# Windowed attention and a gated MLP on one core: the start-up rebuilt around keys that lie four rows to a partition

## The chip, the cores and the metric

The kernel runs on one core of a Trainium2 chip. A core has a matrix engine (TensorE, "PE" in the profile; its weight loads are shown apart as "PEld"), a vector engine (DVE), a scalar engine (ACT), GpSimd (POOL) and a queue engine (SP). [...] The metric is device time in microseconds. Three runs of the kernel before gave 316.60, 316.82 and 317.05 us; the median is 316.82 us.

## The reference

Two stages. The first is attention with 8 batches and 8 heads of 64: per head 512 local rows and 32 global rows. Global queries see all 544 keys; a local query sees the 32 global keys and the local keys at most 32 rows away.

```python
s_g = scale * np.matmul(q_g, k_all.transpose(0, 1, 3, 2))
out_g = np.matmul(sm(s_g), v_all)
s_ll = scale * np.matmul(q_l, k_l.transpose(0, 1, 3, 2))
mask = np.abs(pos[:, None] - pos[None, :]) <= 32
s_ll = np.where(mask, s_ll, -1e9)
s_lg = scale * np.matmul(q_l, k_g.transpose(0, 1, 3, 2))
out_l = np.matmul(sm(np.concatenate([s_lg, s_ll], axis=-1)), np.concatenate([v_g, v_l], axis=2))
```

The second takes the 8 x 544 = 4352 rows of 512 values through `h = x @ w_in` (512 to 2048), `g = h * sigmoid(1.702 h)` and `g @ w_out` (2048 to 512).

## The kernel before, in words

**Tiling.** Four heads of one batch form a quad (`class Quad`, L231), one head on each group of 32 partitions; there are 16 quads, two to a batch (called `a` and `c` in the code). A quad's steps are: `Tk` and `Tq` (L249, L256) transpose keys and queries on DVE in 32x32 blocks; `ext` (L264) puts the 32 global queries beside the local ones; `S(rnd)` (L281) makes the scores of key chunks 0, 1 (round 0) or 2, 3 (round 1), each chunk being 128 keys against the window of queries that can see them; `X(rnd)` (L318) is the exponential on ACT; `M(rnd)` (L329) multiplies with a 0/1 mask on DVE; `K` and `XK` (L334, L358) do the same for the global keys; `ekU(unit)` and `U(unit)` (L362, L385) sum, over keys, the row sums (unit 0) and the two halves of the values (units 1, 2); `R` (L416) turns the row sums into reciprocals on DVE; `XL(h)` (L426) scales; `Gm` and `G` (L400, L429) make the global rows' output.

**MLP.** `h_step(i, fc)` (L474) is four 512-column matmuls of batch i into PSUM, a tanh on ACT and one DVE pass into `gT`; `o_mm` (L481) multiplies with `w_out`. After the start-up PE alternates between `h_step`s of one batch and `phase_o`, which mixes that batch's `o_mm`s with the attention of the next.

**Order.** The order of the work is written out by hand (`manual_schedule`): every engine runs its instructions in the order of the code and waits on semaphores that the framework sets from the data. One further limit: a POOL DMA waits for the eighth one before it to have landed. PSUM has one set of four score banks (`psS`, one buffer) and four single banks (`psP`), so a second `S` in the score banks waits for the `X` of the first.

**Start-up, L119 to L602.** Quad 0's keys and queries come in f32 as four 256 KB loads on the ACT and SP queues (L125 to L127) and are converted on ACT (L520) and DVE (L531); quad 1's come through POOL (L149). Keys lie 16 rows to a partition, and `Tk` writes them with a stride so that the transposed keys are in natural order. PE starts with 40 filler matmuls (L163). The window is not applied by `M` here but by `B` (L272): 32 matmuls of an identity with a table of 0 and -262144 put the bias into the banks before `S` adds the scores. The 0/1 mask for later quads is made on ACT between `h_step`s (L599). Values of the global keys (`g32v`) are loaded on SP only after a DVE memset (`hold`, L109) that stands behind the transposes. `load_rest` (L203) issues the rest from POOL: values of batch 0, `w_in` in six pieces (the first 512 columns first), two of the four pieces of `w_out`, then queries, keys and global rows of quad 2, the other `w_out` pieces, and so on.

**Lines the change touches:** `kf`, `vf` (L65, L66), `load` (L73), `load_g32` (L107), the constants (L131 to L149), `make_mask` (L188), `load_rest`, `Tk`, `B`, `S`, `X`, `M`, and the start-up order from L519 to L616.

Of the kernel before, what the change touches and what calls it, by code (L numbers as in the profile page):

```python
# [12 lines left out]
F32 = mybir.dt.float32  # L13
BF16 = mybir.dt.bfloat16
# [6 lines left out]
def kernel(  # L21
# [43 lines left out]
    kf = k_l.rearrange("b (u j) (r t) d -> b (j r) u (t d)", j=4, t=16)  # L65
    vf = v_l.rearrange("b h (c g r) d -> b g r h c d", c=4, g=4)  # L66
# [6 lines left out]
    def load(b, us=(0, 1), kq=True):  # L73
        if b not in loaded:
            loaded[b] = (ld.tile([128, 2, 16 * D], BF16, name="rk"),
                         ld.tile([128, 2, 16 * D], BF16, name="rq"))
        if kq:
            s = slice(us[0], us[-1] + 1)
            nc.gpsimd.dma_start(out=loaded[b][0][:, s], in_=kf[b][:, s])
            nc.gpsimd.dma_start(out=loaded[b][1][:, s], in_=qf[b][:, s])  # L80
# [3 lines left out]
    def load_v(b, us=(0, 1)):  # L84
        s = slice(us[0], us[-1] + 1)
        hs = slice(4 * us[0], 4 * us[-1] + 4)
        for g in range(4):
            p = slice(32 * g, 32 * g + 32)
            nc.gpsimd.dma_start(out=vtiles[b % 2][p, s, :, :, :D], in_=vf[b, g][:, hs])  # L89
# [17 lines left out]
    def load_g32(name, src, hold=False):  # L107
        t = g32[name] = consts.tile([128, 2, D], F32, name="g32%s" % name)
        if hold:  # L109
            nc.vector.memset(t[:, :, 0:1], 0.0)  # L110
        if name == "v":
            load_turned(nc.sync, t, src[:, 0:2, :])
        else:
            nc.sync.dma_start(out=t, in_=src[:, 0:2, :])

    def cast_g32(name, t):
        nc.vector.tensor_copy(t[:, 0:2, :D], g32[name])  # L117

    load(0, kq=False)  # L119
    rk, rq = loaded[0]  # L120
    k32 = ld.tile([128, 16 * D], F32, name="k32", bufs=1)
    q32 = ld.tile([128, 16 * D], F32, name="q32", bufs=1)
    halves = (slice(0, 8 * D), slice(8 * D, 16 * D))
    load_g32("q", qgf)
    for eng, f in ((nc.scalar, halves[0]), (nc.sync, halves[1])):  # L125
        eng.dma_start(out=k32[:, f], in_=kf[0][:, 0, f])
        eng.dma_start(out=q32[:, f], in_=qf[0][:, 0, f])  # L127
    load_g32("k", kgf)


    step = consts.tile([128, 257], BF16)  # L131
    nc.vector.memset(step, 1.0)
    ones32 = consts.tile([128, 32], BF16)
    nc.gpsimd.memset(ones32, 1.0)
    nc.gpsimd.memset(rvg[:, :, D:], 1.0)
    bd = consts.tile([128, 4, 32], BF16)
    nc.gpsimd.memset(bd, 0.0)
    for j in range(4):
        r = (j + 1) % 4
        nc.gpsimd.memset(bd[32 * r : 32 * r + 32, j, :], 1.0)  # L140
    for i in range(2):
        v = consts.tile([128, 2, 4, 4, D + 2], BF16, name="v%d" % i)
        nc.gpsimd.memset(v[:, :, :, :, D:], 1.0)
        vtiles.append(v)
    nc.gpsimd.affine_select(
        out=step, in_=step, pattern=[[1, 257]], compare_op=ALU.is_ge,
        fill=0.0, base=-65, channel_multiplier=-1,
    )
# [14 lines left out]
    keep(40, psP.tile([128, 512], F32, name="w", tag="p"), 128)  # L163
# [8 lines left out]
    WIN = ((0, 10), (6, 12), (14, 12), (22, 10))  # L172
    mask = consts.tile([128, 2, LW], BF16)


    ident = consts.tile([128, 128], BF16)
    band = consts.tile([128, 192], BF16)
    bias = consts.tile([128, 16, 12], BF16)
    bandt = band.rearrange("p (r t) -> p t r", t=16)
    nc.vector.tensor_sub(ident, step[:, 65:193], step[:, 64:192])  # L180
    nc.vector.tensor_sub(band, step[:, 65:257], step[:, 0:192])
    nc.vector.tensor_scalar(bias, bandt, -1.0, 262144.0, op0=ALU.add, op1=ALU.mult)

    def near(t, c):
        lo = 0 if c else 2
        return t[:, :, lo : lo + WIN[c][1]]

    def make_mask(c):  # L188
        nr = WIN[c][1]
        at = (0, 160, 0, 192)[c]  # L190
        nc.scalar.activation(mask[:, c // 2, at : at + 16 * nr].rearrange("p (t r) -> p t r", t=16),
                             near(bandt, c), AF.Copy)
# [10 lines left out]
    def load_rest():  # L203
        vp = v_l[0].rearrange("(u h) (c p) d -> u p h c d", u=2, p=128)
        for u in range(2):
            for p in (slice(0, 64), slice(64, 128)):
                nc.gpsimd.dma_start(out=vtiles[0][p, u, :, :, :D], in_=vp[u, p])
        half = d_ff // 2
        for part, lo, hi in ((0, 0, 512), (0, 512, half), (1, 0, half)):
            for u in range(2):  # L210
                nc.gpsimd.dma_start(out=w_in_sb[:, part, 2 * u : 2 * u + 2, lo:hi],
                                    in_=w_in_r[u][:, :, part * half + lo : part * half + hi])
        for g4 in (1, 0, 2, 3):
            nc.gpsimd.dma_start(
                out=w_out_sb[:, 4 * g4 : 4 * g4 + 4, :].rearrange("p (g e) m -> p g (e m)", e=2),
                in_=w_out_r[:, 2 * g4 : 2 * g4 + 2, :])
            if g4 == 0:
                load(1, (0,))
                load_g(2, 4)
# [11 lines left out]
    class Quad:  # L231
        def __init__(self, Q):
# [11 lines left out]
            self.bk = {}  # L244
# [4 lines left out]
        def Tk(self, lo=0, hi=16):  # L249
            if lo == 0:  # L250
                self.kT = att.tile([128, Sl], F32, name="kT", bufs=3)
                self.k = self.kT.bitcast(BF16).rearrange("p (m e) -> p m e", e=2)
            nc.vector.transpose(self.kT.rearrange("p (r t) -> p t r", t=16)[:, lo:hi],  # L253
                                loaded[self.b][0][:, self.u].bitcast(F32)[:, 32 * lo : 32 * hi])
# [16 lines left out]

        def B(self, rnd, split=False):  # L272
            self.bk[rnd] = [pbank("s") for _ in range(4)] if split else self.spt(rnd)
            ps = self.bk[rnd] if split else [self.bk[rnd][:, j, :] for j in range(4)]
            for c in (2 * rnd, 2 * rnd + 1):
                w = (40, 200, 36, 228)[c]
                for j in range(4):
                    nc.tensor.matmul(ps[j][:, w : w + 16 * WIN[c][1]], lhsT=ident, rhs=near(bias, c),
                                     start=(c == 2 * rnd), stop=False, skip_group_check=True)

        def S(self, rnd, split=False, added=False, part=None):  # L281
            if not added:
                self.bk[rnd] = self.spt(rnd)
            ps = self.bk[rnd] if split else [self.bk[rnd][:, j, :] for j in range(4)]
            for c in (2 * rnd, 2 * rnd + 1):
                off = (0, 200, 0, 228)[c]
                r0, nr = WIN[c]
                t0, t1 = ((0, 20), (4, 23), (1, 20), (4, 24))[c]
                lo, hi = ((t0, t1) if part is None else (12, t1) if part else (t0, 12))
                off += (lo - t0) * nr  # L290
                n = (hi - lo) * nr
                for e in range(2):
                    for j in range(4):
                        p = slice(32 * j, 32 * j + 32)
                        nc.tensor.matmul(  # L295
                            ps[j][:, off : off + n],
                            lhsT=self.k[p, 128 * c : 128 * c + 128, e],
                            rhs=self.q[p, lo:hi, r0 : r0 + nr, e],
# [484 lines left out]
```

## Time and profile before

| what | value |
|---|---|
| median of three runs | 316.82 us |
| profiled execution, its own time | 316.6 us |
| span of its instructions | 314.9 us |
| PE busy | 302.8 us, 96% |
| DVE busy / ACT busy / POOL busy | 210.5 / 167.5 / 55.9 us |
| PE idle in one piece, 13.19 to 16.33 us | 3.14 us |
| first `h_step` matmul of the dense part (fc = 4) | 26.68 us |
| DMA bytes, mean rate | 27.60 MB, 88 GB/s |
| software queue | 45760 packets, 47.7% of 16 engines' span |

The profile is of one execution; its own time is its span plus 1.7 us around it. "PE busy" is the time in which a matmul is in the array. The chain of waits is followed back from the last instruction: each piece is what released the next one. In it PE has 88% of the span, in two lines above all: L488 (`w_out`, 37%) and L463 (`w_in`, 34%). The "timeline" gives instructions in order of time, and in brackets how long the engine was idle before and who ended that. A table "by stretches" gives the busy time of each engine between two times, the TensorE clock that was granted (1.00 is full) and the DMA rate.

### The profile page before, as it was taken

To read this page: it belongs to the slowest core of one execution; us is meant where nothing else is said; L and a number is where in the kernel's file an instruction comes from. 1 tells how busy PE (TensorE), PEld (TensorE's weight loads), DVE (VectorE), ACT (ScalarE), POOL (GpSimd) and SP (SyncE) were. 2 spreads that over 40 slices of the span, in tenths; PEclk is the share of its full clock that TensorE was granted. 3 is DMA by queue.
4 is the path that set the end of the run, shared out by engine and by line. 5 is a ranking of instruction groups with operands and counts; after the bars stand their busy time and mean duration, and the time that the engine had idled before them with its cause. 6 is when DMAs were issued, how large, how long until landed. Compare 5 with 4: busy or idle time off the path is not lost.

```text
span 314.9 us, 7824 instructions
## 1 busy us (share of the span) xinstructions
PE 302.8 (96%) x3272; PEld 149.9 (48%) x3272; DVE 210.5 (67%) x447; ACT 167.5 (53%) x251; POOL 55.9 (18%) x90
## 2 busy tenths in 40 slices
PE   8599999899999999999999999999999999999994
PEld 7354444444454454544554454444454454446553
DVE  6367865696867767678767876776857865573320
ACT  3725746267355655566546744665456642563421
POOL 8533575630004000500032000300000000000000
PEclk9979999999999999999999999999999999999999
DMA  7999999999139511990159312900211012200222
GB/s 194 176 209 206 202 116 189 213 197 94 33 70 120 115 34 37 104 164 3 44 79 158 60 34 60 111 0 18 53 38 32 2 35 52 51 0 18 51 67 68
DMA packets 53923, 27.60 MB, mean 88 GB/s; under 512 B 42496, under 2 KB 43776, under 8 KB 53888
## 3 DMA queue, kind: packets, MB, share of 16 engines
q0 software_dynamic: 45760, 16.95, 47.7%
q1 hardware_dynamic: 7648, 9.51, 12.2%
q10 hardware_dynamic: 480, 0.66, 0.7%
q8 instruction: 25, 0.41, 0.6%
q14 instruction: 10, 0.08, 0.1%
HBM read 35.13 MB, written 8.91 MB: 140 GB/s over the span
## 4 chain that ended last, share of the span: by engine, by line
PE 88%; DVE 4%; DMA 4%; ACT 2%; issue 0%; ACTq 0%; SPq 0%; DVEq 0%
PE op L488 37%; PE hp L463 34%; PE s L295 6%; PE ov L394 5%; PE ov L372 3%; DMA g32v<-in_v_g_dram 2%; DMA k<-in_k_l_dram 1%; DVE gT L471 1%; PE s L463 1%; PE kb L314 1%; PE op L500 1%; PE s L314 1%; ACT th L470 1%; PE s L412 1%; ACT e L325 1%; DVE kT L253 0%
## 5 line engine op out<-in xcount | busy, mean ns | idle before, releaser
L488 PE MATMUL op<-w_out_sb,gT 128*128 128x512 bf16 x528 | 122.0, 380 | 0.1
L471 DVE SCALAR_TENSOR_TENSOR gT<-th,hp 128x512 bf16<-128x512 f32 (+1 forms) x140 | 91.2, 656 | 43.5 <-ACT th L470 42.6
L463 PE MATMUL hp<-xL,w_in_sb 128*128 128x512 bf16 x496 | 109.0, 379 | 1.0 <-DVE xL L427 1.0
L470 ACT ACTIVATE th<-hp 128x512 f32<-128x512 f32 (+1 forms) x140 | 79.9, 573 | 43.6 <-PE hp L463 39.6
L463 PEld LDWEIGHTS <-w_in_sb 128*128 128x128 bf16 x576 | 56.0, 98 | 66.0 <-issue 2.2
L488 PEld LDWEIGHTS <-gT 128*128 128x128 bf16 x528 | 49.2, 98 | 56.4 <-issue 3.5
L325 ACT ACTIVATE e<-s 128x1712 bf16<-128x1712 f32 x31 | 49.5, 1597 | 19.3 <-PE s L412 8.9
L502 ACT ACTIVATE ob<-op 128x512 f32<-128x512 f32 (+2 forms) x35 | 20.5, 585 | 63.1 <-PE op L488 60.6
L89 POOL DMA_DIRECT2D v<-in_v_l_dram x32 | 23.8, 753 | 124.1 <-PE s L412 114.4
L332 DVE TENSOR_TENSOR e<-e,mask 128x1408 bf16<-128x1408 bf16 x28 | 24.4, 871 | 6.7 <-ACT e L325 6.7
L418 DVE STREAM_TRANSPOSE sT<-ov 128x512 f32<-128x512 f32 x15 | 10.7, 716 | 27.1 <-PE ov L394 27.1
L295 PE MATMUL s<-q,kT 32*128 32x228 bf16 (+5 forms) x528 | 21.3, 283 | 0.8 <-DVE q L267 0.8
L427 DVE TENSOR_TENSOR xL<-ov,rs 128x512 bf16<-128x512 f32 x30 | 19.4, 687 | 2.7 <-PE ov L394 1.4
L295 PEld LDWEIGHTS <-kT 32*128 32x128 bf16 x528 | 11.0, 96 | 14.3 <-issue 10.3
L253 DVE STREAM_TRANSPOSE kT<-rk 128x512 f32<-128x512 f32 (+1 forms) x17 | 16.8, 990 | 1.2 <-ACT rk L521 1.2
L360 ACT ACTIVATE ek<-kb 128x512 bf16<-128x512 f32 x16 | 9.6, 602 | 8.0 <-PE kb L314 8.0
L372 PE MATMUL ov<-ek,rvg 32*32 32x512 bf16 x120 | 9.8, 384 | 3.1 <-DVE rvg L117 3.1
L394 PE MATMUL ov<-e,v 128*32 128x160 bf16 (+1 forms) x480 | 12.6, 243 | 0.0
L422 DVE STREAM_TRANSPOSE rs<-rT 128x512 f32<-128x512 f32 x16 | 11.4, 711 | 0.6
L394 PEld LDWEIGHTS <-v 128*32 128x32 bf16 x512 | 10.1, 98 | 1.6 <-issue 1.6
L257 DVE STREAM_TRANSPOSE q<-rq 128x512 f32<-128x512 f32 (+1 forms) x17 | 10.8, 641 | 0.0
L314 PE MATMUL kb<-q,kgT 32*32 32x512 bf16 x128 | 10.0, 385 | 0.0
(77 smaller groups left out, 163.3 us busy)
## 6 DMA issues: line engine op xcount, KB each, us to landing
out_dram<-ob SPq DMA_DIRECT2D x132, 64.0 KB, 1.7
v<-in_v_l_dram POOLq DMA_DIRECT2D x28, 128.0 KB, 4.8
rk<-in_k_l_dram POOLq DMA_DIRECT2D x6, 512.0 KB, 8.5
rq<-in_q_l_dram POOLq DMA_DIRECT2D x6, 512.0 KB, 10.5
w_out_sb<-in_moe_w_out_dram POOLq DMA_DIRECT2D x4, 512.0 KB, 11.5
w_in_sb<-in_moe_w_in_dram POOLq DMA_DIRECT2D x4, 256.0 KB, 9.7
w_in_sb<-in_moe_w_in_dram POOLq DMA_DIRECT2D x2, 512.0 KB, 12.8
rk<-in_k_l_dram POOLq DMA_DIRECT2D x3, 256.0 KB, 7.9
```

The lines of the kernel that those rows point to most:

```text
L89: nc.gpsimd.dma_start(out=vtiles[b % 2][p, s, :, :, :D], in_=vf[b, g][:, hs])
L295: nc.tensor.matmul(ps[j][:, off : off + n], lhsT=self.k[p, 128 * c : 128 * c + 128, e], rhs=self.q[p, lo:hi, r0 : r0 + nr, e], start=(e == ...
L325: nc.scalar.activation(e[:, :, :RW], self.ps[:, :, :RW], AF.Exp, scale=scale)
L332: nc.vector.tensor_mul(e, e, mask[:, rnd : rnd + 1, :].to_broadcast([128, 4, LW]))
L372: nc.tensor.matmul(ov[32 * j : 32 * j + 32, :], lhsT=lv, rhs=self.ek[p], start=True, stop=False, skip_group_check=True)
L394: nc.tensor.matmul(ov[32 * j : 32 * j + 32, :].rearrange("p (t r) -> p t r", t=16)[:, :, r0 : r0 + nr], lhsT=lv, rhs=self.E[c // 2][:, j, ...
L427: nc.vector.tensor_mul(self.x[:, 2 * self.u + h, :], self.st[1 + h], self.st["rs"])
L463: nc.tensor.matmul(hp[:, : width(i)], lhsT=w_in_c[:, fc // 8, kc, fc % 8 // 2, :, fc % 2], rhs=(xL[i] if i < B else xG)[:, kc, :], start=( ...
L470: nc.scalar.activation(th[:, :n], hp[:, :n], AF.Tanh, scale=0.851)
L471: nc.vector.scalar_tensor_tensor(gTs[i][:, fc, :n], in0=th[:, :n], scalar=1.0, in1=hp[:, :n], op0=ALU.add, op1=ALU.mult)
L488: nc.tensor.matmul(op, lhsT=gTs[i][:, fc, tci * 128 : tci * 128 + 128], rhs=w_out_sb[:, fc, :], start=(first and fc == 4 * f4), stop=(fc = ...
L502: nc.scalar.activation(ob[:, lo:hi], op[:, lo:hi], AF.Copy, scale=0.5)
```

## The change

The keys are laid out four rows to a partition in each chunk of 128 (`kf`), so that `Tk` writes without a stride and the transposed keys are in the order (chunk, row mod 4, row div 4). The values take the same order (`vf`), and the mask is built for it. Every key load becomes four DMAs of 32 partitions from POOL instead of one of 128.

In the start-up, `B` with its 32 matmuls goes, and with it the identity and the bias table. Quads 0 and 1 are masked by `M` on DVE, as all later quads were before; quad 1's round 1 has its `X` in two pieces and its `M` in two. The mask is now made ahead of the first `X`: two selects on POOL, four copies on DVE (`make_mb`), four ACT instructions (`make_mask`). Quad 0's keys come through POOL as the first four DMAs, in bf16; its queries as one 512 KB load on ACT's queue, followed there by `g32v`, now without a hold. Several memsets go from POOL to DVE. PE has 62 filler matmuls at the start and 4, 3 and 4 wider ones before `S(1)`, `ekU(1)` and `ekU(2)`. `S` is no longer cut in two for quad 0. Global rows of quads 2 and 3 come in f32 on SP and are converted on ACT in the middle of the first `h_step`s, instead of four DMAs from POOL; their transposes move there as well. `w_in` comes in four pieces instead of six, and `w_out` in natural order.

```diff
-    kf = k_l.rearrange("b (u j) (r t) d -> b (j r) u (t d)", j=4, t=16)
-    vf = v_l.rearrange("b h (c g r) d -> b g r h c d", c=4, g=4)
+    kf = k_l.rearrange("b (u j) (c r t) d -> b j r u c (t d)", j=4, c=4, t=4)
+    vf = v_l.rearrange("b h (c r t) d -> b t r h c d", c=4, t=4)
...
         if kq:
-            s = slice(us[0], us[-1] + 1)
-            nc.gpsimd.dma_start(out=loaded[b][0][:, s], in_=kf[b][:, s])
-            nc.gpsimd.dma_start(out=loaded[b][1][:, s], in_=qf[b][:, s])
+            for j in (0, 2, 1, 3):
+                for u in us:
+                    load_k(b, u, j)
+            load_q(b, us)
+
+    def load_k(b, u, j):
+        nc.gpsimd.dma_start(out=loaded[b][0][32 * j : 32 * j + 32, u], in_=kf[b, j][:, u])
...
-    load_g32("q", qgf)
-    for eng, f in ((nc.scalar, halves[0]), (nc.sync, halves[1])):
-        eng.dma_start(out=k32[:, f], in_=kf[0][:, 0, f])
-        eng.dma_start(out=q32[:, f], in_=qf[0][:, 0, f])
-    load_g32("k", kgf)
+    nc.scalar.dma_start(out=q32, in_=qf[0][:, 0])
+    load_g32(0, "qk")
+    load_g32(0, "v", eng=nc.scalar)
+    for j in range(4):
+        load_k(0, 0, j)
+
+    mk = consts.tile([32, 208], BF16)
+    nc.vector.memset(mk, 1.0)
+    for sg, base in ((1, 2 * W + 3), (-1, -3)):
+        nc.gpsimd.affine_select(
+            out=mk, in_=mk, pattern=[[-sg, 208]], compare_op=ALU.is_ge,
+            fill=0.0, base=base, channel_multiplier=4 * sg,
+        )
     load(0, (1,))
...
-    keep(40, psP.tile([128, 512], F32, name="w", tag="p"), 128)
+    keep(62, psP.tile([128, 512], F32, name="w", tag="p"), 128)
...
+    def make_mb():
+        for k in range(4):
+            nc.vector.tensor_copy(mb[32 * k : 32 * k + 32],
+                                  mk[:, 3 - k : 195 - k].rearrange("p (r t) -> p t r", t=16))
...
     def load_rest():
...
-        for part, lo, hi in ((0, 0, 512), (0, 512, half), (1, 0, half)):
+        load_v(0)
+        for part in range(2):
+            cs = slice(part * (d_ff // 2), (part + 1) * (d_ff // 2))
             for u in range(2):
...
-        for g4 in (1, 0, 2, 3):
+        for g4 in range(4):
...
-            if g4 == 0:
+            if g4 == 1:
                 load(1, (0,))
-                load_g(2, 4)
...
-            nc.vector.transpose(self.kT.rearrange("p (r t) -> p t r", t=16)[:, lo:hi],
-                                loaded[self.b][0][:, self.u].bitcast(F32)[:, 32 * lo : 32 * hi])
+            rk = loaded[self.b][0][:, self.u].bitcast(F32).rearrange("p c w -> p (c w)")
+            cs = slice(128 * cs[0], 128 * cs[-1] + 128)
+            nc.vector.transpose(self.kT[:, cs], rk[:, cs])
...
+    make_mb()
+    cast_q(0)
+    cast_q(1)
+    make_mask()
+    cast_g32(0, "q")
     transpose_g(0, 2, "q")
     a.ext((0, 1))
-    a.Tk(0, 8)
-    a.Tk(8, 16)
-    nc.vector.tensor_copy(rq[:, 0, halves[1]], q32[:, halves[1]])
     a.Tq(0, 8)
     a.Tq(8, 16)
+    a.Tk((0, 1))
     a.ext((2, 3))
-    load_g32("v", vgf, hold=True)
-    cast_g32("k", rkg)
+    a.Tk((2, 3))
+    cast_g32(0, "k")
     transpose_g(0, 2, "k")
     load_rest()
-    a.B(0)
-    a.B(1, split=True)
-    a.S(0, added=True, part=0)
-    a.S(0, added=True, part=1)
+    a.S(0)
     a.X(0)
-    a.S(1, split=True, added=True)
+    a.S(1, split=True, warm=4)
     a.X(1)
+    c.ext()
+    cast_g32(0, "v")
     c.Tk()
-    c.ext()
-    c.Tq()
-    cast_g32("v", rvg)
-    c.B(0)
     a.K()
     a.XK()
-    c.S(0, added=True)
+    a.M(0)
+    c.Tq()
     c.gg()
+    c.S(0)
     c.X(0)
+    a.M(1)
+    load_g32(1, "qkv", hold=True)
     a.eg()
-    c.K()
+    c.K(0)
+    a.ekU(0)
+    c.K(1)
     c.XK()
-    a.ekU(0)
     a.U(0)
     a.R()
-    a.ekU(1)
+    a.ekU(1, 3)
+    c.S(1)
+    c.X(1, halves=True)
+    a.ekU(2, 4)
     a.U(1)
+    a.U(2)
+    a.Gm()
+    c.M(0)
     a.XL(0)
-    c.B(1)
-    c.S(1, added=True)
-    c.X(1)
-    a.ekU(2)
-    a.U(2)
+    c.M(1, 0, 192)
+    c.M(1, 192)
     a.XL(1)
-    a.Gm()
...
-        if fc in (5, 6, 8, 9):
-            make_mask((5, 6, 8, 9).index(fc))
+        if fc == 7:
+            cast_g32(1, "qkv")
+        if fc == 10:
+            transpose_g(2, 4)
...
     a.T()
-    transpose_g(2, 4)
     a.ext()
```

## The prediction

> **What bounds the kernel now.** The page first: is one engine full, and where is it not?
>
> ```profile
> PE 302.8 (96%) x3272; PEld 149.9 (48%) x3272; DVE 210.5 (67%) x447; ACT 167.5 (53%) x251; POOL 55.9 (18%) x90
> ...
> PE   8599999899999999999999999999999999999994
> ```
>
> PE is full but for the first two slices of 7.9 us and the last. Then the table by stretches:
>
> ```profile
> core 0: us, PE busy (x) PEld busy (x) DVE busy (x) ACT busy (x) POOL busy (x), PEclk, DMA share, GB/s
> 8.00:16.00 8.00, 4.12 (x124) 2.36 (x112) 2.37 (x10) 5.95 (x9) 4.41 (x7) 1.00 1.90 176
> 16.00:23.00 7.00, 6.67 (x145) 3.75 (x146) 4.79 (x10) 1.60 (x1) 2.51 (x4) 0.76 1.16 208
> 27.00:37.00 10.00, 10.00 (x48) 4.51 (x47) 8.52 (x13) 8.84 (x17) 5.54 (x9) 1.00 1.20 206
> 131.00:165.00 34.00, 34.00 (x384) 16.12 (x383) 25.13 (x51) 19.70 (x28) 4.12 (x7) 1.00 0.55 78
> ```
>
> From 27 us PE has no gap to speak of, and the change leaves its work there alone: the time is the moment at which the dense part starts, plus a constant. From 8 to 16 us half of PE's time is idle, and after it the granted clock is 0.76: the idle stretch was paid twice. The chain says what set the start, with its beginnings and lengths in us:
>
> ```profile
> 8.62 7.33 DMA g32v<-in_v_g_dram
> 16.05 0.24 DVE rvg L117
> 16.33 0.40 PE ov L372 x4
> ...
> 17.14 0.95 PE s L278 x8
> 18.10 0.83 PE s L295 x13
> ...
> 22.91 3.56 PE s L463 x16
> ...
> 26.75 10.47 PE hp L463 x48
> ```
>
> A 64 KB load of the global values, issued at 8.62 because of its hold, lands at 15.95 behind the bulk loads; all of DVE's queue (`R` of quad 0 too) and PE's `ekU(1)` stand behind it. The timeline gives two more anchors: when quad 1's row sums start, and the one later stall that belongs to key transposes.
>
> ```profile
> 20.93 0.49 PE L394 MATMUL ov<-e,ones 128*32 128x160 bf16 x16
> ...
> 70.61 0.67 PE L295 MATMUL s<-q,kT 32*128 32x200 bf16 x16 [0.76 <-DVE q L267]
> ```
>
> From 20.93 (`c.U(0)`) to the dense part at 26.68 lie 5.75 us of the same instructions in both kernels. So the question is when `c.U(0)` can start: it needs quad 1's second mask product.
>
> **The first scores.** *Queries.* Four 256 KB loads landed at 3.54, 5.11, 5.54 and 6.76; with the two 64 KB ones 1.13 MB were in at 6.97. The changed kernel has 0.70 MB on these queues (512 KB, three times 64), so by proportion from 1.3 us they are in at 4.8, `g32v` with them. Two conversions at 0.63 (L521): 6.1. Four mask instructions at 0.49 to 0.55: 8.1, free while ACT has no scores to read; without that cover they cost up to their 2.1 us. They leave the `h_step`s, where ACT has 8.84 of 10 us and PE no gap: nothing gained there; the three conversions put in their place (about 0.3 each) are less than what left.
> *POOL.* Four key pieces from 0.80 at 0.55 to 0.69 each (L79), then two selects at no more than 0.40 (L145): mask base at 3.8 to 4.4. The memsets taken from POOL (1.1 us) are about as long on DVE, which was waiting anyway. Four copies at about 0.25 (row L181), conversion, transpose and two `ext` (0.23, 0.24, 0.28): 6.2 at the latest. `Tq` in halves at 0.42: 6.5.
> *Keys.* The last piece is issued at 2.45. How long until it lands is the one unknown that matters. Lower bound 3.5 us (a 128 KB value piece on a quiet queue, issued 93.75), upper bound 8.7 (the value piece issued at 5.99, queued behind others); the first software load here took 5.9 beside 1.13 MB of other loads. I take 4.7, midway between 3.5 and 5.9 since less runs beside it: 7.2. First half of `Tk` without stride, as `Tq` 0.42: scores could start at 7.7. The 62 fillers from 1.53 at 111 ns (40 took 4.45) end at 8.4, or at 7.8 if the clock rises at 7.2 as it seems to do here. I take 8.2.
>
> [...]
>
> **From the first scores to `c.U(0)`.** `S(0)` 0.66 (row at full clock): first `X` at 8.9, where before it was 8.53. Then ACT is the bound, in order: 1.60, quad 0's split `X` 1.81, `XK` 0.65, quad 1's `X` 1.60 with 0.19, its `XK` 0.60, a wait of 0.15 as `c.S(1)` (0.66) needs the score banks, and two half `X` together 1.70: 17.3 us. On DVE the added `M`s cost 0.89 each: quad 0's (12.4 to 13.3) stands ahead of `U(0)` and `R` (1.7), all while ACT is busy; quad 1's first at 15.6; `c.Tq`, moved behind a mask product, ends near 12.3, ahead of `c.X(0)`'s turn at 13.05. What is late next: `XL(0)` must have `U(1)`, which stands behind the four fillers (0.86) after `c.S(1)`: done 17.3, so `XL(0)` to 18.0 (0.69), then the two last pieces of `M` (0.49 and 0.41): 18.95. `c.U(0)` at 19.0, 1.9 us sooner than 20.93. No gap of PE on the way is longer than about 1 us, so I count no half clock. `c.R` now starts behind `XL(1)` at 19.6 and ends the second `XL` at 22.8; the matmuls that need it come at 23.5.
>
> The 32 bias matmuls that go (2.09 for 16, 0.77 and 1.02) count nothing beyond this: the first 24 stood under waits, the last 8 under the path just replaced. The 11 wide fillers stand where PE waits for ACT.
>
> **The loads behind.** POOL has 13 DMAs ahead of `w_in` instead of six, so the last value piece is issued near 9.4 (5.99 before) and the second `w_in` piece near 10.5. But these landings were paced by the transfers, not by the issue: `w_in`'s first half was whole at 20.64; its first piece is now wanted at 20.8, its second at 22.7. The keys move as 512-byte packets instead of 2 KB; bytes are equal. Bound below: no wait; above: lags as long as the longest here, 8.7 for values (18.1 against a use at 16.9) and 13.5 for `w_in` (24.0 against 22.7), at most 1.3 us. I take 0, as the transfers are the same but for order. `w_out`, quads 2 and 3 were 2 to 9 us early, and the four POOL DMAs of global rows are gone there (each waited 0.7 to 1.8 us for its turn). Their f32 loads on SP come at about 14, are wanted after 27, and land 7.3 us later as `g32v` did.
>
> **Later.** Key transposes fall from 1.04 to 0.67 (rows kT and q of 128x512). PE waits for DVE only in places; the 0.76 at 70.61 has one such transpose in DVE's backlog before it: 0.37 less, bounds 0 and 0.37, I take 0.35. Seven more POOL DMAs per batch, at 0.55, find POOL 18% busy.
>
> **Sum.** 316.6 (the profiled run) - 1.9 - 0.35 = 314.35; the median is 0.22 above that run: 314.5 us.
>
> **Rivals.**
> *Keys land late (slower).* If the split keys take the upper lag, 8.7 us, they land at 11.2 and scores start at 11.6 instead of 8.2: 3.4 us, and the fillers having run out some 3 us before, as long an idle stretch as the one that halved the clock here, about 0.7 more: 318.6. For: POOL loads beside others took 5.9 to 8.7 here, and quad 1's keys and queries come later too (`c.Tk` ahead of `M(0)` in DVE's queue). Against: nothing but 0.7 MB is ahead of them. It decides from a lag of about 7 us (scores at 10.4).
> *Values or `w_in` late (about even).* The 1.3 us above: 315.8; with the lag of the keys a little over my value, 316.8.
> *More gained.* If keys come with the quiet lag and DVE gets `M` in ahead of `XL(0)`, `c.U(0)` starts at 17.6: 313.1.
>
> [...]
>
> **How the numbers follow.** A change below 0.2% (0.6 us) can't be told here. Likeliest 0.46 (its own range 313.6 to 315.8); more gained 0.07; values or `w_in` late 0.13, mostly within 0.2%; keys late 0.34, of it 0.32 slower. Faster 0.56, same 0.12, slower 0.32. The range reaches from the gain to the full price of the first rival: 313.2 to 318.6.
>
> **What would show it.** Right: no wait on `g32v`; first `X` at 8.7 to 9.3; ACT without gaps over 0.5 us from there to about 17.3; `c.U(0)` near 19.0 and the dense part near 24.8; granted clock 1.00 from 8 to 27. Wrong: DVE's `Tk` waiting for the key loads past 8, PE idle after the fillers, a clock below 1, or matmuls on L463's successor waiting for `w_in`.

## The result, and the profile after

The changed kernel took 313.82 us (median of 4 runs, 313.68 to 314.48) beside 316.94 us for the kernel before (4 runs, 316.60 to 317.31): a ratio of 0.9906, 95% interval 0.9887 to 0.9924. On another chip it took 313.65 us (6 runs, 313.45 to 313.85) beside 317.27 us (17 runs, 315.99 to 318.68): 0.9890, 0.9864 to 0.9916. The forecast was 314.5 us.

The profiled execution took 313.87 us, with a span of 312.2 us. First the page of the changed kernel, PE's busy time and its 40 slices:

```profile
PE 303.3 (97%) x3257; PEld 149.2 (48%) x3257; DVE 210.8 (68%) x463; ACT 167.3 (54%) x254; POOL 79.9 (26%) x131
...
PE   8899999899999999999999999999999999999995
```

The second slice is now 8 where it was 5. The table by stretches of the same kernel (busy time and, in brackets, instructions of each engine, granted clock, DMA share, rate):

```profile
core 0: us, PE busy (x) PEld busy (x) DVE busy (x) ACT busy (x) POOL busy (x), PEclk, DMA share, GB/s
8.00:16.00 8.00, 7.14 (x131) 3.21 (x131) 6.80 (x21) 6.82 (x10) 7.12 (x11) 1.00 1.63 150
16.00:23.00 7.00, 6.37 (x128) 3.17 (x128) 5.80 (x14) 0.86 (x2) 1.51 (x4) 1.00 1.12 196
27.00:37.00 10.00, 10.00 (x48) 4.48 (x46) 8.61 (x15) 7.20 (x15) 4.77 (x8) 1.00 1.17 207
```

From 8 to 16 us DVE is busy for 6.80 us (2.37 before) and PE for 7.14 (4.12 before; up to 2.8 of the 7.14 are the 11 wide fillers). From 16 to 23 the granted clock is 1.00 where it was 0.76. From 27 to 37 us PE has no gap in either kernel; ACT's mask instructions are gone from that stretch (7.20 us against 8.84).

The wait itself, first in the kernel before: DVE idle for 5.65 us until the load has landed, and PE for 3.14 us behind DVE's conversion.

```profile
16.05 0.23 DVE L117 CAST rvg<-g32v 128x128 bf16<-128x128 f32 x1 [5.65 <-DMA g32v<-in_v_g_dram]
...
16.33 0.40 PE L372 MATMUL ov<-ek,rvg 32*32 32x512 bf16 x4 [3.14 <-DVE rvg L117]
```

In the changed kernel the same conversion waits for nothing:

```profile
9.02 0.22 DVE L132 CAST rvg<-g32v 128x128 bf16<-128x128 f32 x1
```

The 64 KB of `g32v` go as two DMAs. What landed at 15.95 before was the second, of 16 KB; the first, of 48 KB, was issued at 8.24 and landed at 15.36.

The timeline of PE around the two anchors of the forecast, `c.U(0)` (L391, `ones`) and the dense part (L460, `hp`), and the later place with key transposes:

```profile
17.58 0.34 PE L391 MATMUL ov<-e,ones 128*32 128x160 bf16 x8
18.12 0.66 PE L391 MATMUL ov<-e,ones 128*32 128x192 bf16 x8 [0.20 <-DVE e L329]
...
22.40 1.90 PE L460 MATMUL s<-xL,w_in_sb 128*128 128x512 bf16 x8 [0.29 <-DMA w_in_sb<-in_moe_w_in_dram]
...
24.51 3.85 PE L460 MATMUL hp<-xL,w_in_sb 128*128 128x512 bf16 x17
...
68.31 0.67 PE L291 MATMUL s<-q,kT 32*128 32x200 bf16 x16 [0.63 <-DVE q L273]
```

The second half of `c.U(0)` waits 0.20 us for DVE's mask product; nothing waits for `g32v`. The dense part starts at 24.51 instead of 26.68: 2.17 us. A new wait is there, 0.29 us for the second piece of `w_in`, and it is what the chain of waits now follows:

```profile
10.41 0.69 POOL w_in_sb L219
11.10 11.25 DMA w_in_sb<-in_moe_w_in_dram
...
22.40 1.90 PE s L460 x8
```

The rest of the span differs little. At 70.61 (before) and 68.31 (after) the distance is 2.30, as the wait there fell from 0.76 to 0.63; PE's last matmul ends at 310.61 and 308.37, which is 2.24 sooner. The span is 2.73 shorter (314.89 and 312.16), so 0.49 lies behind the last matmul. There stand the last stores of the output; the DMA view near the end gives for the four of 24 KB, first of the kernel before, then of the changed one:

```profile
out_dram<-ob SPq DMA_DIRECT2D x2, 24.0 KB, 2.0
out_dram<-ob ACTq DMA_DIRECT2D x2, 24.0 KB, 2.2
```

```profile
out_dram<-ob SPq DMA_DIRECT2D x2, 24.0 KB, 1.5
out_dram<-ob ACTq DMA_DIRECT2D x2, 24.0 KB, 1.6
```

The last number is the time from issue to landing: half a microsecond less, for the same stores with no load left beside them (the last DMA from POOL, the page's software queue, was issued more than 100 us earlier, at 197). It does not take the whole change: in experiment 1's profile, the kernel before with one load moved, the same four landed after 1.58 to 1.75 us.

### The profile page after: what moved, and what is told of

The parts are those of the page before. It is cut to its first block, busy times and chain, and to the rows that moved or that the text cites. A ratio compares the mean times of both kernels' runs of the same rounds, so it can differ in the third digit from the quotient of the medians.

```text
span 312.2 us, 7885 instructions
## 1 busy us (share of the span) xinstructions
PE 303.3 (97%) x3257; PEld 149.2 (48%) x3257; DVE 210.8 (68%) x463; ACT 167.3 (54%) x254; POOL 79.9 (26%) x131
## 4 chain that ended last, share of the span: by engine, by line
PE 87%; DMA 4%; DVE 3%; POOL 3%; ACT 2%; issue 1%; ACTq 0%; POOLq 0%; DVEq 0%
PE op L485 37%; PE hp L460 34%; PE s L291 5%; PE ov L391 4%; DMA w_in_sb<-in_moe_w_in_dram 4%; PE ov L369 2%; POOL rk L84 1%; DVE gT L468 1%; PE kb L310 1%; POOL v L97 1%; PE op L497 1%; PE s L310 1%; PE s L460 1%; ACT th L467 1%; PE s L409 1%; ACT e L322 1%
## 5 line engine op out<-in xcount | busy, mean ns | idle before, releaser
L460 PE MATMUL hp<-xL,w_in_sb 128*128 128x512 bf16 x496 | 109.0, 379 | 1.0 <-DVE xL L424 1.0
L460 PEld LDWEIGHTS <-w_in_sb 128*128 128x128 bf16 x576 | 55.9, 98 | 66.6 <-issue 2.2
L322 ACT ACTIVATE e<-s 128x1712 bf16<-128x1712 f32 (+2 forms) x32 | 49.6, 1552 | 15.1 <-PE s L409 8.9
L97 POOL DMA_DIRECT2D v<-in_v_l_dram x36 | 26.9, 754 | 97.4 <-PE s L409 88.8
L84 POOL DMA_DIRECT2D rk<-in_k_l_dram x64 | 34.8, 554 | 12.4 <-DMA w_in_sb<-in_moe_w_in_dram 5.5
L329 DVE TENSOR_TENSOR e<-e,mask 128x1408 bf16<-128x1408 bf16 (+2 forms) x33 | 28.0, 852 | 7.6 <-ACT e L322 7.4
L291 PE MATMUL s<-q,kT 32*128 32x200 bf16 (+1 forms) x512 | 21.3, 284 | 1.2 <-DVE q L273 0.6
L391 PE MATMUL ov<-e,v 128*32 128x160 bf16 (+1 forms) x480 | 12.1, 239 | 0.0
L260 DVE STREAM_TRANSPOSE kT<-rk 128x512 f32<-128x512 f32 (+1 forms) x17 | 11.4, 670 | 0.0
L391 PEld LDWEIGHTS <-v 128*32 128x32 bf16 x512 | 10.0, 97 | 1.1 <-issue 1.1
```

Of the source, the lines that this page charges most:

```text
L84: nc.gpsimd.dma_start(out=loaded[b][0][32 * j : 32 * j + 32, u], in_=kf[b, j][:, u])
L291: nc.tensor.matmul(ps[j][:, off : off + n * nr], lhsT=self.k[p, 128 * c : 128 * c + 128, e], rhs=self.q[p, t0 : t0 + n, r0 : r0 + nr, e], ...
L322: nc.scalar.activation(e[:, :, lo:hi], self.ps[:, :, lo:hi], AF.Exp, scale=scale)
L329: nc.vector.tensor_mul(e, e, mask[:, rnd : rnd + 1, lo:hi].to_broadcast([128, 4, hi - lo]))
L391: nc.tensor.matmul(ov[32 * j : 32 * j + 32, :].rearrange("p (t r) -> p t r", t=16)[:, :, r0 : r0 + nr], lhsT=lv, rhs=self.E[c // 2][:, j, ...
L460: nc.tensor.matmul(hp[:, : width(i)], lhsT=w_in_c[:, fc // 8, kc, fc % 8 // 2, :, fc % 2], rhs=(xL[i] if i < B else xG)[:, kc, :], start=( ...
```

## The experiments

No kernel below leaves any work out; each computes everything that the reference asks for. They ran in three groups on three chips, each beside the kernel before (317.04, 317.53 and 317.27 us); a ratio is to that group's runs of it. Ratios and intervals are those on record; they differ from the quotient of the medians by up to 0.0033.

**1. The held load alone, on the kernel before.** The change has many parts; the forecast names one thing as what set the start before, the 64 KB of global values that landed at 15.95.

```diff
...
     load_g32("k", kgf)
+    load_g32("v", vgf, eng=nc.scalar)
...
-    load_g32("v", vgf, hold=True)
```

> The kernel before with one thing altered: the global values of quads 0 and 1 (g32v) are loaded on ACT's queue right behind the first two key and query loads, without the hold, as the changed kernel does. Theory A (the late g32v was what the start-up before waited for): it lands near 7 us, the 3.14 us of idle PE at 13.19 goes, the granted clock stays at 1.00, quad 1's second scores come near 14.5 instead of 18.1, its row sums near 17.4 instead of 20.93 as nothing has to be masked, the dense part starts near 23.2 instead of 26.68: 313.4 us, as fast as the changed kernel or a little faster. Theory B (the gain came from the rest: no bias matmuls, keys by POOL, mask products, fillers): the wait is taken over by the next thing (values of batch 0, landing at 14.7, or the bias matmuls in the score banks) and at most 1 us is gained: 315.9 or more.

Measured: 312.87 us (10 runs, 312.70 to 315.35), ratio 0.9886, 0.9855 to 0.9918. As far as the intervals can tell, this one edit brings as much as the whole change (0.9887 to 0.9924). Its timeline and stretches:

```profile
17.06 0.34 PE L395 MATMUL ov<-e,ones 128*32 128x160 bf16 x8
17.60 0.34 PE L395 MATMUL ov<-e,ones 128*32 128x192 bf16 x8 [0.20 <-ACT e L326]
...
23.20 5.14 PE L464 MATMUL hp<-xL,w_in_sb 128*128 128x512 bf16 x23
```

```profile
8.00:16.00 8.00, 6.61 (x172) 4.13 (x171) 5.45 (x18) 6.00 (x10) 4.01 (x7) 1.00 1.72 180
16.00:23.00 7.00, 6.80 (x125) 3.24 (x124) 4.65 (x11) 1.55 (x1) 2.96 (x5) 1.00 1.16 208
```

`c.U(0)` starts at 17.06 and the dense part at 23.20, sooner than in the changed kernel, and the half clock is gone without any added filler. In this kernel the bias matmuls stay, so nothing of DVE stands between quad 1's exponential and its row sums.

**2. The held load put back into the changed kernel.** The converse: `g32v` is loaded late, on SP behind a memset, and converted behind `c.Tq`.

```diff
-    load_g32(0, "v", eng=nc.scalar)
...
     a.Tk((2, 3))
+    load_g32(0, "v", hold=True)
...
-    cast_g32(0, "v")
...
     c.Tq()
+    cast_g32(0, "v")
```

> The changed kernel with g32v late again: on SP behind a held memset that stands after the second half of Tk, and its conversion behind c.Tq as before. Theory A: it is issued near 8.3 and lands near 15.5; R of quad 0 starts at 17 instead of 13.5, the dense part at 28 instead of 24.5: 317.3 us, about the time of the kernel before or more. Theory B: at most 1 us is lost, 314.8.

Measured: 315.45 us (10 runs, 314.66 to 318.42), ratio 0.9978, 0.9940 to 1.0015: against 0.9906 the gain is mostly gone, and what is left of the change can't be told from nothing (by the medians alone, 315.45 beside 317.04, half a per cent would be left). The profiled execution is the longest of the ten (318.42 us):

```profile
14.79 0.23 DVE L132 CAST rvg<-g32v 128x128 bf16<-128x128 f32 x1 [2.35 <-DMA g32v<-in_v_g_dram]
14.94 0.89 DVE L328 TENSOR_TENSOR e<-e,mask 128x1408 bf16<-128x1408 bf16 x1
...
15.88 0.45 PE L390 MATMUL ov<-e,ones 128*32 128x192 bf16 x5 [1.88 <-DVE g32v L120]
```

```profile
8.00:16.00 8.00, 4.60 (x101) 2.23 (x104) 4.54 (x18) 6.02 (x9) 7.17 (x11) 0.94 1.67 151
16.00:23.00 7.00, 7.00 (x103) 2.66 (x99) 3.27 (x6) 1.66 (x2) 1.71 (x4) 0.58 1.09 194
```

It is the picture of the kernel before: DVE waits 2.35 us for the load, the mask product stands behind it, PE 1.88 us behind that, and then the clock is 0.58. This execution, in which the load landed at 14.70, took longer than the expected 317.3 us, and its dense part starts at 29.32. That the median is lower has to do with the other runs, which divide by their mean granted clock: the five at 0.999 and 1.000 took 314.66 to 315.08 us, the five at 0.987 to 0.995 took 315.82 to 318.42. None of the first five was profiled, so where the load landed in them is not known; without a half clock the late load cost the changed kernel some 1.2 us (median 314.89, beside 313.82 and 313.65 on other chips).

**3. The same one edit on the other queue.** `g32v` behind `g32k` on SP, where it stands behind all of quad 0's own loads.

```diff
     load_g32("k", kgf)
+    load_g32("v", vgf)
...
-    load_g32("v", vgf, hold=True)
```

> The kernel before with g32v straight behind the last early load on SP, without the hold, in place of ACT's queue as in the first experiment. Theory A: queries no longer share the queues with it and are whole near 6.8 instead of 7.4, the scores of quad 0 start 0.4 us sooner, g32v still lands by 8.5; the dense part near 22.8: 312.5 us. If the order of the early loads is worth nothing: as the first experiment, 312.9.

Measured: 313.03 us (6 runs, 312.59 to 313.86), ratio 0.9867, 0.9837 to 0.9897. In its profile the scores start at 7.86 and the dense part at 22.85. That seemed clearly better than the change; so both were run on one chip.

**4. The change and the one edit side by side.** The changed kernel:

> The changed kernel itself, beside the best one-edit version on the same chip. If the whole change is worth less than the one edit (the early load of the global values), it measures a ratio near 0.991 here and the one-edit version near 0.987, about 1.2 us apart. If the two verdicts only differed because they were taken on different chips or in different landings of the loads, the two lie within 0.2% of one another.

and the kernel of experiment 3:

> The kernel before with only the load of the global values moved: behind the global keys on SP's queue, no hold. Theory A (the one edit is the gain, the rest of the change gives some of it back): ratio 0.985 to 0.989, some 313.0 us, and below the changed kernel by 0.5 to 1.5 us. Rival (both gain the same 0.9%, the rest of the change is worth nothing either way): ratio 0.990 to 0.992.

Measured: the change 313.65 us (6 runs, 313.45 to 313.85), ratio 0.9890 (0.9864 to 0.9916); the one edit 313.37 us (6 runs, 312.69 to 316.72), ratio 0.9898 (0.9857 to 0.9939). The medians lie 0.28 us apart, inside what can be told, and the expected 0.5 to 1.5 us were not there. So the edit alone brings what the change brings; that the rest of the change takes something back is not shown. What differs is the spread: the changed kernel's ten runs lie within 1.03 us, the twelve of the one edit within 4.1, of which one run of 316.72 makes most (the other eleven lie within 1.73). A profiled run of the one edit that took 314.32 us shows one way in which it varies:

```profile
7.54 0.43 DVE L532 CAST rq<-q 128x512 bf16<-128x512 f32 x1 [0.71 <-DMA q<-in_q_l_dram]
```

The second half of quad 0's queries landed at 7.52 (6.58 in the profile of experiment 3), the scores started at 8.38 instead of 7.86, the mean clock from 10.30 to 17.10 was 0.75 (1.00 in experiment 3's), and the dense part began at 24.43 instead of 22.85. The changed kernel has its queries in at 4.74 and 5.21 in its two profiles. In the five profiles of it and its variants the first scores start at 7.91 or 7.92, in the nine of the kernel before and its variants anywhere from 7.79 to 10.08. Steady first scores alone do not make a steady time, though: the variant of experiment 5 has them too, and its ten runs reach from 313.23 to 317.05 us.

**5. What the new wait for `w_in` costs.** Six pieces as before, in the changed kernel.

```diff
-        for part in range(2):
-            cs = slice(part * (d_ff // 2), (part + 1) * (d_ff // 2))
+        half = d_ff // 2
+        for part, lo, hi in ((0, 0, 512), (0, 512, half), (1, 0, half)):
...
```

> The changed kernel with w_in in six pieces again, the first 512 columns first. If the 0.29 us that PE waited at 22.11 for the second w_in piece is all that the loads cost: the first 512 columns are whole near 19, the wait goes, 0.3 us less: 313.5. If smaller pieces and two more POOL issues cost as much: 313.8, no difference.

Measured: 314.31 us (10 runs, 313.23 to 317.05), ratio 0.9947, 0.9914 to 0.9981: no gain. The wait is gone (the four pieces that are wanted first landed at 16.94 to 21.80), but in the profile another load is late, quad 1's queries, landed at 12.02 instead of 10.94:

```profile
12.81 0.66 PE L292 MATMUL s<-q,kT 32*128 32x200 bf16 x16 [1.38 <-DVE q L264]
```

Whether the six pieces caused that or it was this execution's landing is open; the 0.29 us are not worth having at this price.

**6. The wide fillers.** The changed kernel without the 4 + 3 + 4 wide ones.

```diff
-    a.S(1, split=True, warm=4)
+    a.S(1, split=True)
...
-    a.ekU(1, 3)
+    a.ekU(1)
...
-    a.ekU(2, 4)
+    a.ekU(2)
```

> The changed kernel without the 11 wide filler matmuls of the start-up (the 62 narrow ones at its begin stay). If they keep the clock up: PE has some 2.5 us more of idle time between 8 and 17, the granted clock falls to half for a window of 3.4 us, 0.7 to 1.7 us are lost: 314.5 to 315.5. If they only fill waits: U(1) and XL(0) come 0.8 us sooner and the last mask product with them, 0 to 0.5 us gained: 313.3 to 313.8.

Measured: 313.92 us (10 runs, 313.27 to 314.83), ratio 0.9911, 0.9884 to 0.9938: the same as with them. In its profile the clock does fall, and the dense part still starts at 24.07, 0.44 sooner than in the changed kernel's:

```profile
8.00:16.00 8.00, 6.04 (x124) 2.71 (x124) 6.25 (x21) 6.51 (x10) 6.72 (x11) 0.79 1.67 149
```

From 8 to 16 us ACT is the busiest engine (6.51 of 8 us), which would leave slower matmuls little to cost there; and the four fillers that stood ahead of `U(1)`, and with it ahead of `XL(0)`, are gone. Whether these two effects cancel was not separated, and the profiled execution is the fastest of the ten (313.27 us).

**7. Is it the wait or the half clock that costs before?** The kernel before, with 14 wide fillers ahead of the matmuls that wait.

```diff
-    a.ekU(1)
+    a.ekU(1, 14)
```

> The kernel before with 14 wide filler matmuls in the idle stretch from 13.19 to 16.33, g32v as late as ever: the clock alone. Theory C (half of the loss is the halved clock after the wait): granted clock 1.00 from 16 to 23, the dense part 0.6 to 1.2 us sooner: 315.8 to 316.4. Theory A in its pure form (the wait is all, what PE does after it is bound by ACT and DVE): at most 0.3 us, 316.7.

Measured: 316.96 us (12 runs, 315.96 to 319.75), ratio 0.9995, 0.9970 to 1.0020: nothing gained, and inconclusive. In the profiled run (319.12 us, mean clock 0.989) `g32k` was late: the matmuls that read its transpose waited for it and started at 10.74, where in the kernel before they started at 8.89. The matmuls were slow before the fillers began at 16.50 (eight bias matmuls at 11.30 took 1.33 us, and 0.77 at 10.18 in the kernel before), and the fillers then stood in the way of real work until 19.86. The runs of the kernel before say more. Over the 67 of them, the mean granted clock goes with the time: 33 runs under 0.990 took 317.10 to 318.70 us, the 7 at 0.997 took 314.86 to 316.18. In the profile of the kernel before the clock is 0.50 from 17.47 to 20.88, and these 3.41 us take 0.0054 off the mean of its span. By an estimate from that one stretch, 0.989 is two of them and 0.997 is less than one. If so, the seven runs at 0.997 had the held load and no such stretch, and they are still 2.0 to 3.3 us above the one edit on their own chips (312.87 and 313.03): the greater part of its gain of 4.2 to 4.5 us is there without the clock. How the rest divides is open, as in the profiles of the kernel before and of experiment 2 a late `g32v` came with both a longer wait and a half clock.

**8. Mask products in place of bias matmuls, on the one edit.** Experiment 3's kernel with the change's other main part: `M` for quads 0 and 1, masks before the first `X`, halves of `X` and `M` in quad 1's round 1, quad 1's `S(1)` ahead of `XL(0)`, and no `B`.

```diff
+    for cc in range(4):
+        make_mask(cc)
...
-    a.B(0)
-    a.B(1, split=True)
-    a.S(0, added=True, part=0)
-    a.S(0, added=True, part=1)
+    a.S(0, part=0)
+    a.S(0, part=1)
...
-    c.B(0)
+    a.M(0)
...
+    a.M(1)
...
+    c.S(1)
+    c.X(1, halves=True)
+    c.M(0)
     a.XL(0)
-    c.B(1)
-    c.S(1, added=True)
-    c.X(1)
...
+    c.M(1, 0, 192)
+    c.M(1, 192)
...
```

> As the one on SP above, but with no bias matmuls at all: the mask is made ahead of the first exponential and all four rounds of quads 0 and 1 take mask products on DVE, quad 1's last in two pieces with two half exponentials, as in the changed kernel; keys and loads as before. What the mask's way is worth by itself: quad 1's last scores come 0.75 sooner without bias, the last product costs 0.4 to 0.9 behind the exponential, and four mask instructions just fit ahead of the first exponential: within 0.5 us of it, 312.3 to 313.2. If the products are what holds the changed kernel back against the first experiment (24.5 against 23.2): 1.3 us slower, 313.8.

Measured: 315.42 us (8 runs, 314.09 to 316.20), ratio 0.9935, 0.9908 to 0.9962, beside 313.03 us and 0.9867 of experiment 3 on the same chip: this part alone costs 2.4 us. In its profile PE is idle for 2.41 us ahead of the first scores, since nothing fills the place of the bias matmuls, and the clock is halved from 8.86 to 15.69; quad 1's last row sums wait for the mask product:

```profile
8.19 1.46 PE L296 MATMUL s<-q,kT 32*128 32x120 bf16 x48 [2.41 <-DVE q L258]
...
18.36 0.66 PE L396 MATMUL ov<-e,ones 128*32 128x192 bf16 x8 [0.41 <-DVE e L334]
...
24.29 1.90 PE L465 MATMUL hp<-xL,w_in_sb 128*128 128x512 bf16 x8
```

**9. The same with the change's fillers.** 75 narrow ones at the start, 4 wide ones ahead of `S(1)`, 3 ahead of `ekU(1)`.

```diff
-    keep(40, psP.tile([128, 512], F32, name="w", tag="p"), 128)
+    keep(75, psP.tile([128, 512], F32, name="w", tag="p"), 128)
...
+            if split:
+                keep(4, ps[0])
...
-    a.ekU(1)
+    a.ekU(1, 3)
```

> The early load of the global values, with mask products in place of bias matmuls, as in the earlier kernel that lost 2.4 us against the one edit alone, but now with filler matmuls as in the change: 75 narrow ones at the start, 4 wide ones before S of quad 0's round 1, 3 before ekU(1). Theory C (that loss was the half clock of 8.86 to 15.69 us, which followed PE's idle stretch of 2.41 us): no half clock, quad 1's last exponential by 15.9, dense part near 23.3 to 23.6, ratio near 0.989. Theory D (the products and the four mask instructions themselves are the loss, because they stand in DVE's and ACT's queues ahead of the scores): dense part near 24.2 again, ratio near 0.9935, whatever the clock.

Measured: 314.01 us (6 runs, 313.79 to 316.14), ratio 0.9917, 0.9884 to 0.9949. It lies between the two theories, and its interval holds both. It ran on another chip than experiment 8, so the two medians are compared with care; beside the one edit on its own chip (313.37 us, 0.9898) it costs 0.64 us where experiment 8 cost 2.4, and the intervals overlap. The profile has the clock at 1.00 from 8 to 23 us and yet a dense part at 24.95, later than in experiment 8, for another reason:

```profile
10.64 0.23 DVE L117 CAST rkg<-g32k 128x128 bf16<-128x128 f32 x1 [1.64 <-DMA g32k<-in_k_g_dram]
```

`g32k` landed at 10.62, and keys, queries and masks of quad 1 stood behind its conversion. So theory C as I wrote it falls in this execution: a full clock did not bring 23.6. In experiment 8, too, the three runs at a clock of 1.00 took 315.25, 315.60 and 316.20 us, and the five at 0.986 to 0.989 took 314.09 to 316.04. What the products cost by themselves stays open.

**10. The product for one quarter only.** Experiment 3's kernel with halves and mask products in quad 1's round 1 alone.

```diff
+    make_mask(2)
+    make_mask(3)
...
-    c.B(1)
-    c.S(1, added=True)
-    c.X(1)
+    c.S(1)
+    c.X(1, halves=True)
...
+    c.M(1, 0, 192)
+    c.M(1, 192)
```

> As the one on SP above, bias matmuls for three of the four rounds, where PE is idle anyway, and the two half exponentials with mask products for quad 1's last round alone, where the bias stands on the path: 0.75 less ahead of the exponential, 0.4 more behind it: 0.3 us sooner, 312.2, the fastest of all. If DVE has no room for the two pieces between R and XL there: no gain, 312.5 or more.

Measured: 313.63 us (6 runs, 312.36 to 315.04), ratio 0.9885, 0.9850 to 0.9920: no gain over 0.9867. Its profiled execution is well above its median (314.82 us, `g32k` landed at 10.37), so the profile can't say what the halves are worth.

**11. Global keys ahead of the second halves.** `g32k` was late in several profiles, so here it goes ahead of the second halves of keys and queries on SP. The expectation speaks of fillers as well; the kernel that ran has only this reordering of experiment 3's kernel and no added filler, so it is read as that.

```diff
     load_g32("q", qgf)
+    load_g32("k", kgf)
     for eng, f in ((nc.scalar, halves[0]), (nc.sync, halves[1])):
         eng.dma_start(out=k32[:, f], in_=kf[0][:, 0, f])
         eng.dma_start(out=q32[:, f], in_=qf[0][:, 0, f])
-    load_g32("k", kgf)
     load_g32("v", vgf)
```

> The one-edit version with the global keys loaded on SP ahead of the second halves of keys and queries instead of behind them (in its profile the conversion of the global keys waited 0.23 us for them, landed 8.75; in a sister run 1.46 us, landed 10.37), and with 75 narrow and 4 + 3 wide fillers so that PE has no long idle stretch. If late global keys and half clocks make the spread of this start-up: 0 to 0.5 us sooner than the one-edit version, near 312.6, ratio near 0.986, and a smaller spread. If the 64 KB ahead of the second halves only pushes those back (0.2 to 0.5 us on the scores): ratio near 0.988 to 0.990.

Measured: 316.87 us (12 runs, 316.19 to 318.15), ratio 0.9991, 0.9972 to 1.0010. The whole gain is gone, in every run, by moving one 64 KB load forward; far more than the 0.2 to 0.5 us of the pessimistic expectation. DVE, PE and the stretches:

```profile
9.24 0.43 DVE L532 CAST rq<-q 128x512 bf16<-128x512 f32 x1 [1.68 <-DMA q<-in_q_l_dram]
```

```profile
10.08 1.58 PE L296 MATMUL s<-q,kT 32*128 32x120 bf16 x48 [2.38 <-DVE q L258]
```

```profile
7.00:10.30 3.30, 0.92 (x25) 0.80 (x24) 1.62 (x5) 0.43 (x1) 1.83 (x3) 1.00 1.37 187
10.30:17.10 6.80, 5.99 (x119) 3.22 (x112) 2.82 (x13) 5.00 (x7) 3.69 (x7) 0.50 1.73 183
```

The second half of the queries, issued at 2.33 instead of 1.80 to 1.82, landed at 9.22 instead of 6.58 (experiment 3) or 7.52 (experiment 4): it is now issued at the same time as quad 1's 256 KB of keys from POOL, which landed at 9.40. Whether that neighbour or the 64 KB ahead of them holds the queries up was not separated. Scores start at 10.08 instead of 7.86, PE has been idle for 2.38 us, and the clock is 0.50 from 10.30 to 17.10. The span is 3.9 us longer than in experiment 3.

## Why the prediction was right

The mechanism that the forecast put first is the one the runs show: `g32v` taken out of the hold. Put back (experiment 2), the gain goes; alone on the kernel before (experiments 1, 3, 4), it brings ratios of 0.9867 to 0.9898, the whole of it. The time came out 0.7 us below the forecast's 314.5, in terms as follows.

- *First scores at 8.2*: 7.91, and the first `X` at 8.63 instead of 8.9. The keys landed at 5.49, 5.88, 6.08 and 6.35 us, lags of 4.1 to 3.3, where I took 4.7; the four masks took 1.07 us together, where I had 2.1. So neither was the limit: DVE's queue was, with the mask copies, which waited for POOL's selects, and PE waited 0.18 us for the first half of `Tk`:

```profile
4.54 1.35 DVE L180 COPY mb<-mk 32x192 bf16<-32x192 bf16 x4 [1.03 <-POOL mk L146]
...
7.91 0.66 PE L291 MATMUL s<-q,kT 32*128 32x200 bf16 x16 [0.18 <-DVE kT L260]
```

- *ACT back to back to 17.3*: it ended at 16.86, with one gap of 0.49. That is 0.27 from the earlier start and 0.17 within, 0.1 of it a slip: the terms added to 8.9 give 17.2.
- *`c.U(0)` at 19.0*: the last piece of `M` ended at 18.47 where I had 18.95, behind `XL(0)`, as forecast (16.91 to 17.60), and the second half of the row sums followed (its first half had started at 17.58). From there 5.75 us to the dense part would be 24.22; it started at 24.51. Of the rival *more gained* the first condition came, keys with the quiet lag, and the second did not, as `M` stood behind `XL(0)`: 313.82 lies between its 313.1 and the forecast.
- *`w_in` at no cost, bounds 0 and 1.3*: 0.29. The piece landed at 22.36, 11.25 us after its issue. The rival *values or `w_in` late* came in small, and with it one of the signs that were named as wrong. The 2.17 at the dense part are 2.46 less this 0.29.
- *Key transposes 0.35, bounds 0 and 0.37*: this term failed in size. A transpose of 128x512 did fall from 1044 to 704 ns (medians of 15), but the wait at that place fell from 0.76 only to 0.63. The copies behind it (L273) set the end, and over five profiles of kernels with the new key order the wait was 0.47 to 0.77, over nine with the old one 0.76 to 0.79: between nothing and 0.3 us.
- *The rest of the change at nothing*: the 11 wide fillers bring nothing that can be measured (experiment 6); I had counted them as free, which holds. That the clock stayed at 1.00 came as forecast, but the length of PE's longest gap, by which I judged it, does not tell it in these profiles: a gap of 1.38 us left the clock full in experiment 5's, and in experiment 7's the longest from 6 us to the slow matmuls at 11.30 was 1.01 (see the last section).
- *What was not in the sum*: 0.49 us behind the last matmul. In the five profiles of the changed kernel and its variants, the span ends 3.67 to 3.79 us after the last matmul; in the nine of the kernel before and its variants 4.03 to 4.28. The variants with mask products (experiments 8 to 10) keep the longer end, so it doesn't go with these; nothing in my working speaks of the end, and no experiment was made on it.

Sum: 2.17 + 0.13 + 0.49 less about 0.06 along the way are the 2.73 us of the span. Without the 0.49 it would be 2.24, beside the 2.25 that I had added up; that they agree so closely is luck, as 0.56 more on the way to `c.U(0)` stands against 0.29, 0.22 and 0.06 lost.

The rival *keys late* did not come, since the pieces landed 3.3 to 4.1 us after their issue. Its price was of the right kind but low, as far as a neighbouring kernel tells: in experiment 11 scores that came 2.22 us later than in experiment 3, with PE idle before them and the half clock behind them, cost 3.9 us of span, where my terms (the delay and 0.7) give 2.9. My sum let the four key pieces overlap, with one lag behind the last issue, and that held: issued 0.53 to 0.66 us apart, they landed 0.20 to 0.39 apart. A key piece cost POOL 0.55 us on average (554 ns over 64), and 0.54 to 0.67 for the first eight, beside DVE's memsets and copies; I had taken 0.55 to 0.69.

The expectation that I formed after experiments 1, 3 and 8, that the change's other parts give some of the gain back, fell to 0.28 us on one chip (experiment 4). In the changed kernel these parts come with earlier queries, POOL-loaded keys and fillers, and with all of it they even out; which of them would steady the time was not tested.

## What to carry to other kernels

Before a start-up is rebuilt, read who waits for the last-landing small load and undo that alone: one moved load brought here what the whole diff brought. In the first ten microseconds don't price an added or moved load by its bytes alone: look at what it pushes back and what it is then issued beside, as 64 KB put ahead cost 3.5 us here. And compare spreads as well as medians: of two start-ups whose medians could not be told apart, one repeated within 1 us and the other varied by 4.

## What the runs showed of the hardware that I had not expected

- PE's first matmuls were slower than later ones of the same form, up to a moment that differs between executions. In the changed kernel's profile a filler took 310 to 312 ns up to 6.6 us and 220 from 7.1 on; in that of the kernel before a bias matmul 160 columns wide took 341 ns between 5.7 and 6.9 us and 232 between 7.1 and 7.8. The same last 31 narrow fillers, from 4.75 us on, took 2.98, 1.96, 2.29 and 2.41 us in the profiles of the changed kernel and of experiments 2, 5 and 6.
- The granted clock was 0.50 for stretches of 3.41 us in the kernel before (17.47 to 20.88) and 3.4 in experiments 4 and 6 (0.75 of 6.8 us, 0.79 of 8), some 6.8 in experiments 2, 8 and 11 (in the last, 0.50 from 10.30 to 17.10). Gaps on PE of 3.14 us (the kernel before), 2.41 (experiment 8), 2.38 (experiment 11) and 1.45 (experiment 6) came ahead of half clock, while 1.21 in experiment 1 and 1.38 in experiment 5 left it full; but in experiment 7 the matmuls were slow at 11.30 with no gap above 1.01 between 6 us and then. What decides it was not shown.
- A 256 KB load on SP's queue (the second half of quad 0's queries), issued 0.51 us later, landed 2.6 us later (9.22 in experiment 11, 6.58 in experiment 3); it was then issued together with a POOL load of the same size.
- The same small load landed anywhere between 7.0 and 10.6 us (`g32k`, issued at the same place in the queue in several kernels), with all that stands behind its conversion; it was 6.97 in the kernel before and 10.62 in experiment 9. In experiment 7, whose only edit comes later, the matmuls on its transpose started 1.85 us later than in the kernel before (10.74 and 8.89). The kernel before varies by 3.8 us (314.86 to 318.70 over 67 runs); how much of that such landings make was not measured.
- The last stores of the output land in 1.5 to 1.6 us in the changed kernel and in 2.0 to 2.2 in the kernel before. What makes the difference is open: kernels that keep the longer end (experiments 1 and 8) have short landings too.
